# A padded row pitch for the V table in DRAM: 4608 bytes instead of 4160

## The chip, the core and the metric

The kernel runs on one core of one Trainium2 chip. The metric is device time in microseconds (us) of one execution. A core has a matrix engine (TensorE, "PE" in the profile; its weight loads are "PEld"), VectorE ("DVE"), ScalarE ("ACT"), GpSimd ("POOL") and SyncE ("SP"), which here only issues transfers, and 16 DMA engines that carry all transfers of the core. A matrix instruction reads SBUF and writes PSUM; DRAM is reached by DMA alone.

## What is computed

Block-sparse attention followed by a two-layer network with an ELU in between. From the reference, cut:

```python
B, H, S, D = 4, 8, 768, 64            # q, k, v: [B, H, S, D], float32
scores = q @ k^T / sqrt(D)            # per batch and head
# blocks of 32 positions, 24 of them; block i sees blocks i-1, i, i+1, the first, the last,
# and three blocks drawn at random for it (sampled_blocks[i]); blocks 0 and 23 see everything
attn = softmax(where(mask, scores, -1e9))
x = (attn @ v) as [B*S, H*D]          # 3072 x 512
h = x @ w_in                          # 512 -> 2048
out = where(h > 0, h, exp(min(h, 0)) - 1) @ w_out      # 2048 -> 512
```

## The kernel before, in words

The two batches of a pair and the two halves of a float32 number (a float16 high part and a float16 rest) are handled together. The work is cut into 24 units of attention (12 for each pair of batches; a unit has 128 query rows: two blocks of 32 for each of two batches) and 12 groups of the network (two units each). Units 0 to 3 and the first groups come while the weights are still being loaded, split and stored.

**The V table.** `vd[g]` in DRAM (L582, one for each pair of batches) holds V in the form in which the matrix engine reads it: 832 rows, one for a position; a row has both batches, all 8 heads, and for each the high part, two columns of ones and the rest: `2 * RW = 2080` float16 numbers, 4160 bytes. Row 0 to 31 are zero rows (for sampled blocks that are seen already), the first and the last block stand at the end of the table, and rows 736 to 767 are zero too (block 23's place in the sequence). It is written once:

- `zero_rows` (L584) clears a piece of SBUF (`ST`) and writes the zero rows of both tables with four transfers (L590).
- `first_values` (L648) splits V of the first pair in SBUF (`VT`) and writes it with five transfers (L666), two neighbouring rows, 8320 bytes, for each partition.
- `values` (L681) does the same for the second pair later, a row for each partition (L696).

It is read for every unit (`attention`, L733): for each of the two blocks of a unit one transfer on SP's queue brings the three neighbouring blocks (L803, 96 rows), and one indirect transfer that POOL issues brings 96 rows by their numbers in `idx` (L808). Two more direct transfers (L801, L802) bring the first and last block when a buffer is first used for a pair of batches. The two units that hold blocks 0 and 23 read the table whole (unit 0 from SBUF, unit 18 by L783 to L786). `idx` is built by `tables` (L441), the row number of each lane, as an integer.

**The order.** `Plan` is a list scheduler that runs when the program is built: each operation has the engines it may run on, estimated times and a priority, and the plan writes them down in the order in which a simulated machine would start them. Each engine then runs its list in order. SP's list is the order of the transfers in its queue; at most eight of SP's transfers are under way, since each waits for the one eight places before it (semaphores `DMAHW0` to `DMAHW7`).

At the start SP's list is: the sampled blocks, q of unit 0, eight loads of K (L621), six of V (L612; both in pieces of 512 bytes), the four writes of zero rows (L590), the first piece of `w_in` (L531) and of `w_out` (L535), the five writes of V (L666), three more q's, and so on. A piece of the weights is 1 MB and arrives as float32; `weights` (L504) turns it into two float16 halves: `wu` (L542, written by the helper at L393 on ACT), `ws` (L547), `wg` (L555), `wb` (L559) and so on.

Of the kernel before, what the change touches and what calls it, by code (L numbers as in the profile page):

```python
# [318 lines left out]
def kernel(  # L319
# [10 lines left out]
    nc = tc.nc  # L330
# [7 lines left out]
    NKC = S // P  # L338
    VW = 2 * D + 2
    RW = H * VW  # L340
    ROWS = (NB + 2) * BLK
    KW = (NR + 2) * BLK
    NPAIR = B // 2
# [97 lines left out]
    def tables():  # L441
        room = sb.tile([P, DM], F32, tag="ro.0", name="room")
        raw = room[:, 0 : 2 * NB * NR].bitcast(I32).rearrange("p (a b c) -> p a b c", b=NR, c=2)
        nc.sync.dma_start(
            raw.rearrange("p a b c -> p (a b c)"),
            sampled.bitcast(I32).rearrange("a b -> (a b)").partition_broadcast(P))
        t = room[:, 2 * NB * NR : 2 * NB * NR + 9 * NB].rearrange("p (a b) -> p a b", b=NB)
        sf = t[:, 0:3].rearrange("p a b -> p (a b)").rearrange("p (a b) -> p a b", b=NR)
        own, me, ok, k32 = t[:, 3], t[:, 4], t[:, 5], t[:, 6, 0:1]
        mi, ki = t[:, 7].bitcast(I32), t[:, 8, 0:1].bitcast(I32)  # L450
        nc.gpsimd.iota(mi, pattern=[[1, NB]], base=0, channel_multiplier=0)
        nc.gpsimd.iota(ki, pattern=[[0, 1]], base=0, channel_multiplier=1)
        nc.vector.tensor_copy(me, mi)
        nc.vector.tensor_scalar(ki, ki, BLK - 1, None, op0=ALU.bitwise_and)
        nc.vector.tensor_copy(k32, ki)
        nc.vector.tensor_copy(sf, raw[:, :, :, 0])
        nc.vector.tensor_scalar(
            col16[0:1, :].rearrange("p (a b) -> p a b", b=NR), sf[0:1], float(BLK // 2), None,
            op0=ALU.mult)
        for g in range(P // BLK):  # L460
            rs = slice(BLK * g, BLK * (g + 1))
            nc.vector.tensor_copy(own[rs], sf[rs, :, min(g, NR - 1)])
        nc.vector.tensor_tensor(me, own, me, op=ALU.subtract)
        nc.vector.tensor_tensor(me, me, me, op=ALU.mult)
        nc.vector.tensor_scalar(ok, me, WINDOW + 0.5, None, op0=ALU.is_gt)
        for e in (0.0, NB - 1.0):
            nc.vector.scalar_tensor_tensor(ok, own, e, ok, op0=ALU.not_equal, op1=ALU.mult)
        for g in range(1, NR):
            rs = slice(BLK * g, BLK * (g + 1))
            for r in range(g):  # L470
                nc.vector.tensor_tensor(me[rs], own[rs], sf[rs, :, r], op=ALU.not_equal)
                nc.vector.tensor_tensor(ok[rs], ok[rs], me[rs], op=ALU.mult)
        nc.vector.scalar_tensor_tensor(own, own, float(BLK), ok, op0=ALU.mult, op1=ALU.mult)
        nc.vector.tensor_scalar(idx, own, k32, None, op0=ALU.add)

    def turn16(t, src, dst, via, new=(), w=(), name="", bank="s", ml=ML):

# [101 lines left out]
    kT_buf = [[fixed(kT[:, :, x, c * P : (c + 1) * P]) for c in range(NKC)] for x in range(2)]  # L579
    kT_any = [b for x in kT_buf for b in x]  # L580
    kT_head = [Buf(None, None) for _ in range(H // 2)]
    vd = [buf("vd", [ROWS, 2 * RW], F16, dr) for _ in range(NPAIR)]  # L582

    def zero_rows(prio):  # L584
        z = spot("st4", lambda i: ST[:, i].bitcast(F16))
        plan.add({"POOL": 0.6}, prio, lambda e: nc.gpsimd.memset(z.ap[0:BLK, :], 0.0), new=[z], name="zero", port=False)
        for b in range(NPAIR):
            for n in (0, NB - 1):
                def put(e, b=b, n=n):
                    nc.sync.dma_start(vd[b].ap[n * BLK : (n + 1) * BLK, :], z.ap[0:BLK, :])  # L590
                plan.add({"SP": 0.45}, prio, put, r=[z], new=[vd[b]] if n == 0 else [],
                         w=[] if n == 0 else [vd[b]], dma=0.47, name=f"z{b}", pk=32)

# [54 lines left out]
    def first_values(a, js, prio, load, write):  # L648
        def slot():
            assert next_slot() == a  # L650
            return VT[:, 2 * a : 2 * a + 2].rearrange("p c b (h x) -> p c b h x", h=H)
        n = Buf("VT", slot)
        v_room.append(n)
        plan.add({"POOL": 0.5}, prio - 3, lambda e: nc.gpsimd.memset(
            n.ap.rearrange("p c b h x -> p (c b h) x")[:, :, D : D + 2], 1.0), new=[n], name=f"v10.{a}", port=False)
        for x in range(2):
            s, t = staged(js[x], v[x], a, load, f"v0.{a}")
            for c in range(2):
                split(prio, s, n, lambda x=x, c=c: n.ap[:, c, x, :, 0:D],
                      lambda x=x, c=c: n.ap[:, c, x, :, D + 2 :], VS, False, f"v0.{a}", t[:, :, c, :], mh=MHO)  # L660
        last = NB // (2 * P // BLK) - 1
        pieces = {0: [(0, HB, NB * BLK), (HB, P, BLK)],
                  last: [(0, P - HB, 2 * P * a), (P - HB, P, (NB + 1) * BLK)]}.get(a, [(0, P, 2 * P * a)])
        for p0, p1, row in pieces:
            def put(e, p0=p0, p1=p1, row=row):
                nc.sync.dma_start(  # L666
                    vd[0].ap[row : row + 2 * (p1 - p0), :].rearrange("(p c) e -> p (c e)", c=2),
                    n.ap[p0:p1].rearrange("p c b h x -> p (c b h x)"))
            mark["vs"] = plan.add({"SP": 0.43}, write, put, r=[n], w=[vd[0]], dma=2.7 * (p1 - p0) / P, name=f"vs0.{a}",
                     pk=256 * (p1 - p0) // P)  # L670

# [9 lines left out]
    def values(g, c, prio):  # L681
        n = spot("st4", lambda i: ST[:, i].bitcast(F16).rearrange("p (b h x) -> p b h x", b=2, h=H))
        plan.add({"POOL": 0.15}, prio, lambda e: nc.gpsimd.memset(n.ap[:, :, :, D : D + 2], 1.0),
                 new=[n], name=f"v1{g}.{c}", port=False)
        for x in range(2):
            s = buf("st2", [P, H, D], F32)
            plan.add({"SP": 0.9}, prio, lambda e, s=s, x=x: nc.sync.dma_start(
                s.ap, v[2 * g + x][:, c * P : (c + 1) * P, :].rearrange("h p d -> p h d")),
                new=[s], dma=2.0, name=f"v{g}.{c}", pk=1024)
            split(prio, s, n, lambda x=x: n.ap[:, x, :, 0:D], lambda x=x: n.ap[:, x, :, D + 2 :],  # L690
                  VS, False, f"v{g}.{c}")
        pieces = {0: [(0, BLK, NB * BLK), (BLK, P, BLK)],
                  NKC - 1: [(0, P - BLK, c * P), (P - BLK, P, (NB + 1) * BLK)]}.get(c, [(0, P, c * P)])
        for p0, p1, row in pieces:
            def put(e, p0=p0, p1=p1, row=row):
                nc.sync.dma_start(  # L696
                    vd[g].ap[row : row + p1 - p0, :], n.ap[p0:p1].rearrange("p b h x -> p (b h x)"))
            plan.add({"SP": 0.45}, prio, put, r=[n], w=[vd[g]], dma=1.8 * (p1 - p0) / P, name=f"vs{g}.{c}")


# [32 lines left out]
    def attention(u, t, via, due):  # L733
# [34 lines left out]
        elif sp:  # L768
# [7 lines left out]
            for c in range(NKC):  # L776
                vt = vts[c // 2]

                def load(e, c=c, vt=vt):
                    dst = VV[vt.slot][:, c % 2].rearrange("p b x -> p (b x)")  # L780
                    r0 = BLK + c * P
                    if c < NKC - 1:
                        nc.sync.dma_start(dst, vd[g].ap[r0 : r0 + P, :])  # L783
                    else:
                        nc.sync.dma_start(dst[0:64], vd[g].ap[r0 : r0 + 64, :])
                        nc.sync.dma_start(dst[64:P], vd[g].ap[NB * BLK :, :])  # L786
                plan.add({"SP": 0.5}, tv, load, r=[vd[g]], w=[vt], dma=1.9, name=f"vt{u}",
                         nd=1 if c < NKC - 1 else 2)
            vin = vts
        else:  # L790
            for y in range(2):
# [4 lines left out]
                def load(e, i=i, vt=vt, y=y):  # L796
                    vt.slot = 3 + y if u == spare else next_slot()
                    two = VV[vt.slot].rearrange("p c b x -> p c (b x)")
                    if in_room.get(("v", vt.slot)) != g:
                        in_room["v", vt.slot] = g  # L800
                        nc.sync.dma_start(two[96:P, 0, :], vd[g].ap[NB * BLK : (NB + 1) * BLK, :])  # L801
                        nc.sync.dma_start(two[0:BLK, 1, :], vd[g].ap[(NB + 1) * BLK :, :])  # L802
                    nc.sync.dma_start(two[BLK:P, 1, :], vd[g].ap[(i - 1) * BLK : (i + 2) * BLK, :])  # L803
                whole = u < spare + 2 or u == spare + 2 and y == 0
                plan.add({"SP": 1.5 if whole else 0.6}, tv, load, r=[vd[g]], new=[vt], dma=2.4 if whole else 1.45,  slack=RANK["SLACK"][2], name=f"vt{u}", nd=3 if whole else 1)

                def gather(e, i=i, vt=vt):
                    nc.gpsimd.indirect_dma_start(  # L808
                        VV[vt.slot][0:96, 0].rearrange("p b x -> p (b x)"), None, vd[g].ap,
                        bass.IndirectOffsetOnAxis(ap=idx[0:96, i : i + 1], axis=0))  # L810
                mark["vt", u] = plan.add({"POOL": 1.0}, tv, gather, r=[vd[g]], w=[vt], dma=1.65, slack=RANK["SLACK"][2], name=f"vg{u}")

# [377 lines left out]
```

## Time and profile before

| | |
|---|---|
| median of 3 runs | 736.94 us (734.59 to 737.84) |
| the profiled execution's own time | 739.45 us |
| its span, first to last instruction | 737.7 us |
| mean granted clock of TensorE | 0.964 |
| PE busy | 686.1 us (93%) |
| PEld, DVE, ACT, POOL busy | 461.7, 505.8, 442.2, 200.8 us |
| bytes moved | 125.26 MB, mean 170 GB/s |

The span begins with the first instruction, and all times inside the trace count from there. The 1.75 us between the span and the execution's own time lie around it. Share and busy time of an engine are means over stages with different limits, so the page's 40 slices and the stretches in the rows below say more.

### The profile page before, as it was taken

To read this page: it belongs to the slowest core of one execution; us is meant where nothing else is said; L and a number is where in the kernel's file an instruction comes from. 1 tells how busy PE (TensorE), PEld (TensorE's weight loads), DVE (VectorE), ACT (ScalarE), POOL (GpSimd) and SP (SyncE) were. 2 spreads that over 40 slices of the span, in tenths; PEclk is the share of its full clock that TensorE was granted. 3 is DMA by queue.
4 is the path that set the end of the run, shared out by engine and by line. 5 is a ranking of instruction groups with operands and counts; after the bars stand their busy time and mean duration, and the time that the engine had idled before them with its cause. 6 is when DMAs were issued, how large, how long until landed. Compare 5 with 4: busy or idle time off the path is not lost.

```text
span 737.7 us, 23053 instructions
## 1 busy us (share of the span) xinstructions
PE 686.1 (93%) x9377; PEld 461.7 (63%) x9377; DVE 505.8 (69%) x933; ACT 442.2 (60%) x867; POOL 200.8 (27%) x413
## 2 busy tenths in 40 slices
PE   7787666999999999999899899999999999999996
PEld 4565444866567677568468468576577477586662
DVE  7989698899988845758678657568466568352140
ACT  6886687786676744448458547546467456363340
POOL 2515226326513320410463323320033242100000
PEclk9689797999999999999999999999999999999999
DMA  9999979788889979788999897898659899621001
GB/s 235 312 282 267 296 216 240 173 190 186 223 129 209 193 184 223 161 200 128 204 139 186 134 201 170 129 212 165 112 99 218 166 167 191 137 44 23 21 1 28
DMA packets 221946, 125.26 MB, mean 170 GB/s; under 512 B 189008, under 2 KB 201424, under 8 KB 221456
## 3 DMA queue, kind: packets, MB, share of 16 engines
q1 hardware_dynamic: 216912, 106.22, 69.4%
q0 software_dynamic: 4928, 17.57, 9.3%
q8 instruction: 73, 1.20, 0.7%
q14 instruction: 33, 0.27, 0.1%
HBM read 76.99 MB, written 13.21 MB: 122 GB/s over the span
## 4 chain that ended last, share of the span: by engine, by line
PE 71%; DVE 8%; DMA 8%; ACT 5%; issue 4%; SPq 2%; POOL 1%; POOLq 1%; ACTq 0%; DVEq 0%
PE h L1057 29%; PE o L1083 26%; PE av L971 5%; PE s L883 5%; DMA pT<-p 2%; PE s L1083 2%; DMA VT<-vd 1%; ACT pT L393 1%; DMA wo<-in_k_dram 1%; DMA VT<-vd,idx 1%; DMA wi<-in_moe_w_in_dram 1%; DVE m L893 1%; DVE FE L1065 1%; SPq L621 1%; PE s L486 1%
## 5 line engine op out<-in xcount | busy, mean ns | idle before, releaser
L1057 PE MATMUL h<-xT,wi 128*128 128x256 f16 x2304 | 267.7, 274 | 3.1 <-DVE wi L566 1.6
L1057 PEld LDWEIGHTS <-wi 128*128 128x128 f16 x2304 | 223.2, 98 | 44.1 <-issue 6.6
L1083 PE MATMUL o<-wo,GR 128*128 128x512 f16 x1008 | 231.4, 379 | 1.3 <-ACT ro L393 0.7
L1083 PEld LDWEIGHTS <-GR 128*128 128x128 f16 x1152 | 108.1, 98 | 124.6 <-issue 7.7
L845 POOL COPY kG<-kT 128x128 int32 x264 | 94.6, 395 | 225.6 <-PE s L883 170.9
L1065 DVE SCALAR_TENSOR_TENSOR FE<-h,FE 128x512 f32<-128x512 f32 x96 | 65.7, 686 | 60.4 <-ACT FE L1070 60.3
L1068 ACT ACTIVATE FE<-h 128x512 f32<-128x512 f32 x96 | 56.8, 592 | 78.0 <-PE h L1057 77.8
L893 DVE TENSOR_REDUCE m<-s 128x2 f32<-128x512 f32 x112 | 75.1, 684 | 40.7 <-PE s L883 40.2
L919 ACT ACTIVATE e<-s,m 128x256 f32<-128x256 f32 x192 | 80.2, 471 | 19.3 <-DVE p L951 16.5
L393 ACT ACTIVATE GR<-FE 128x512 f16<-128x512 f32 x93 | 58.5, 629 | 43.4 <-DVE FE L1065 40.2
L1075 DVE TENSOR_TENSOR GR<-FE,GR 128x512 f16<-128x512 f32 x89 | 61.5, 694 | 26.7 <-ACT GR L393 26.0
L951 DVE TENSOR_TENSOR p<-e,p 128x512 f16<-128x512 f32 x81 | 57.6, 712 | 24.2 <-ACT p L393 19.8
L971 PEld LDWEIGHTS <-pT 128*32 128x32 f16 (+1 forms) x3816 | 49.3, 101 | 38.4 <-issue 35.3
L808 POOL DMA_INDIRECT VT<-vd,idx x42 | 45.3, 1078 | 96.6 <-PE av L971 76.1
L1070 ACT ACTIVATE FE<-FE,gs 128x512 f32<-128x512 f32 x96 | 69.2, 722 | 2.2
L971 PE MATMUL av<-VT,pT 128*32 128x66 f16 (+5 forms) x3624 | 57.8, 206 | 9.1 <-issue 5.3
L393 ACT ACTIVATE p<-e 128x512 f16<-128x512 f32 x74 | 46.1, 626 | 19.4 <-DMA pT<-p 19.2
L883 PE MATMUL s<-kG,qT 128*32 128x256 f16 x704 | 45.2, 281 | 5.8 <-ACT e L919 3.0
L883 PE MATMUL s<-kG,qS 128*32 128x256 f16 x704 | 44.7, 280 | 1.2 <-issue 0.7
L883 PEld LDWEIGHTS <-qT 128*32 128x32 f16 (+1 forms) x816 | 27.6, 100 | 27.0 <-issue 21.1
L393 ACT ACTIVATE ro<-o 128x512 f32<-128x512 f32 x19 | 11.3, 595 | 52.8 <-PE o L1083 52.8
L906 ACT ACTIVATE m<-m 128x2 f32<-128x2 f32 x91 | 18.3, 202 | 34.2 <-DVE m L893 31.0
(141 smaller groups left out, 683.6 us busy)
## 6 DMA issues: line engine op xcount, KB each, us to landing
VT<-vd SPq DMA_DIRECT2D x42, 390.0 KB, 7.2
st<-in_q_dram SPq DMA_DIRECT2D x44, 128.0 KB, 3.5
out_dram<-ro SPq DMA_DIRECT2D x44, 128.0 KB, 2.9
wi<-in_moe_w_in_dram SPq DMA_DIRECT2D x4, 1024.0 KB
wo<-in_k_dram SPq DMA_DIRECT2D x8, 384.0 KB, 6.3
wo<-in_v_dram SPq DMA_DIRECT2D x6, 512.0 KB, 6.9
wo<-in_moe_w_out_dram SPq DMA_DIRECT2D x3, 1024.0 KB, 5.1
st<-in_v_dram SPq DMA_DIRECT2D x12, 256.0 KB, 3.6
```

The source lines that it names most:

```text
L393: nc.scalar.activation(dst, src, AF.Copy, scale=scale)
L845: nc.gpsimd.tensor_copy(dst[:, :, r * 16 : (r + 1) * 16], src[:, :, bass.ds(at[r], 16)])
L883: nc.tensor.matmul(dst, lhsT=qq.ap[:, h, rs], rhs=mv, start=first, stop=(y == 1 and qq is qS and o0 + w == 256))
L893: nc.vector.tensor_reduce(m.ap[:, 2 * c : 2 * c + 2] if sp else m.ap[:, 6:8], ss[c].ap, axis=AX.X, op=ALU.max, negate=True)
L919: nc.scalar.activation(e32.ap[:, y, :], ss[c].ap[:, y, :], AF.Exp, bias=m.ap[:, 6 + y : 7 + y], scale=SC)
L951: plan.add(LO, t + step * hp + 1, margin=mo, fn=lambda e, got=got, p=p: ENG[e].tensor_tensor(p.ap[:, 1, :], got(), p.ap[:, 0, :], op=ALU.s ...
L971: nc.tensor.matmul(av[half].ap[rs, at : at + w], lhsT=pts[c].ap[:, pl * 4 + y * 2 + z, rs], rhs=room[:, z, x, h * VW + v0 : h * VW + v0 + ...
L1057: nc.tensor.matmul(h.ap[:, a, :], lhsT=w[:, wl, cs], rhs=x.ap[:, xl, cc, :], start=(n == 0), stop=(n == 3 * NCC - 1))
L1065: nc.vector.scalar_tensor_tensor(e32.ap, h.ap, -IH * GS, e32.ap, op0=ALU.mult, op1=ALU.min)
L1070: plan.add({"ACT": 0.72}, p0, lambda e: nc.scalar.activation(e32.ap, e32.ap, AF.Relu, bias=gs_col, scale=-GS), r=[e32], w=[e32], name=f"a2 ...
L1075: plan.add(LO, p0, margin=mo, fn=lambda e: ENG[e].tensor_tensor(g.ap[:, 1], e32.ap, g.ap[:, 0], op=ALU.subtract), r=[e32, g], w=[g], name= ...
L1083: nc.tensor.matmul(o.ap, lhsT=g.ap[:, gl, f % 2, m * P : (m + 1) * P], rhs=wo[:, part, wl, (f % 2) * DM : (f % 2 + 1) * DM], start=(f == 0 ...
```

## The change

A row of the table takes 2304 float16 numbers (`FAR`, 4608 bytes, nine times 512) in place of 2080; the 224 numbers (448 bytes) behind each row are padding. All reads and writes of rows take the first 2080 numbers of a row, so that every row that is moved begins at a multiple of 512 bytes (both tables begin at one before and after). The indirect transfers see the table in steps of 256 numbers, and `idx` holds nine times the row number: the last instruction of `tables` multiplies by 9 in the same instruction that adds. `zero_rows` issues one more transfer for each table, which writes zeros into the padding of all 832 rows. The writes of the first pair's V now have two pieces of 4160 bytes for each partition in place of one of 8320.

```diff
+    FAR = -(-2 * RW // 256) * 256
...
-        nc.vector.tensor_scalar(idx, own, k32, None, op0=ALU.add)
+        nc.vector.tensor_scalar(idx, own, k32, float(FAR // 256), op0=ALU.add, op1=ALU.mult)
...
-    vd = [buf("vd", [ROWS, 2 * RW], F16, dr) for _ in range(NPAIR)]
+    vd = [buf("vd", [ROWS, FAR], F16, dr) for _ in range(NPAIR)]
...
-                    nc.sync.dma_start(vd[b].ap[n * BLK : (n + 1) * BLK, :], z.ap[0:BLK, :])
+                    nc.sync.dma_start(vd[b].ap[n * BLK : (n + 1) * BLK, 0 : 2 * RW], z.ap[0:BLK, :])
+                    if n == 0:
+                        nc.sync.dma_start(
+                            vd[b].ap[:, 2 * RW :].rearrange("(p a) e -> p a e", p=BLK),
+                            z.ap[0:BLK, 0 : FAR - 2 * RW].unsqueeze(1).to_broadcast([BLK, ROWS // BLK, FAR - 2 * RW]))
...
-                    vd[0].ap[row : row + 2 * (p1 - p0), :].rearrange("(p c) e -> p (c e)", c=2),
-                    n.ap[p0:p1].rearrange("p c b h x -> p (c b h x)"))
+                    vd[0].ap[row : row + 2 * (p1 - p0), 0 : 2 * RW].rearrange("(p c) e -> p c e", c=2),
+                    n.ap[p0:p1].rearrange("p c b h x -> p c (b h x)"))
...
-                        nc.sync.dma_start(dst, vd[g].ap[r0 : r0 + P, :])
+                        nc.sync.dma_start(dst, vd[g].ap[r0 : r0 + P, 0 : 2 * RW])
...
-                        VV[vt.slot][0:96, 0].rearrange("p b x -> p (b x)"), None, vd[g].ap,
+                        VV[vt.slot][0:96, 0].rearrange("p b x -> p (b x)"), None, vd[g].ap.rearrange("r (a b) -> (r a) b", b=256),
```

The other transfers of rows (L696, L785, L786, L801 to L803) change as the one of L783 above. The estimates of the plan are untouched, and the order on PE, DVE, ACT and POOL is the same, instruction for instruction. SP's list gains the two transfers into the padding. Before, from the last load of V to the second write of V on SP (what a transfer writes, what it reads, its shape, and what SP waits for; `vd_425` and `vd_445` are the tables of the two pairs):

```order
L612 DMA wo<-in_v_dram 128x8x128 [waits DMAHW2_49,DVE_49]
L590 DMA vd_425<-ST 32x2080 [waits DMAHW3_49,Pool_49]
L590 DMA vd_445<-ST 32x2080 [waits DMAHW4_49]
L590 DMA vd_425<-ST 32x2080 [waits DMAHW5_49]
L590 DMA vd_445<-ST 32x2080 [waits DMAHW6_49]
L531 DMA wi<-in_moe_w_in_dram 128x4x512 [waits DMAHW7_49,PE_49]
L535 DMA wi<-in_moe_w_out_dram 128x2x1024 [waits DMAHW0_49,PE_49]
L666 DMA vd_425<-VT 112x4160 [waits DMAHW1_49,DVE_49]
```

With the change, the same stretch (the second table is now called `vd_446`, and lines from L339 on stand one to five further down):

```order
L617 DMA wo<-in_v_dram 128x8x128 [waits DMAHW2_49,DVE_49]
L591 DMA vd_425<-ST 32x2080 [waits DMAHW3_49,Pool_49]
L593 DMA vd_425<-ST 832x1x224 [waits DMAHW4_49]
L591 DMA vd_446<-ST 32x2080 [waits DMAHW5_49]
L593 DMA vd_446<-ST 832x1x224 [waits DMAHW6_49]
L591 DMA vd_425<-ST 32x2080 [waits DMAHW7_49]
L591 DMA vd_446<-ST 32x2080 [waits DMAHW0_49]
L532 DMA wi<-in_moe_w_in_dram 128x4x512 [waits DMAHW1_49,PE_49]
L536 DMA wi<-in_moe_w_out_dram 128x2x1024 [waits DMAHW2_49,PE_49]
L671 DMA vd_425<-VT 224x1x2080 [waits DMAHW3_49,DVE_49]
```

Two transfers of 832 pieces each now stand ahead of the first piece of `w_in`; everything behind them keeps its order and waits on semaphores two places further round.

## Rows read from the trace of the kernel before

**Rows 1.** The page's head, engines and 40 equal slices of the span.

```profile
span 737.7 us, 23053 instructions
PE 686.1 (93%) x9377; PEld 461.7 (63%) x9377; DVE 505.8 (69%) x933; ACT 442.2 (60%) x867; POOL 200.8 (27%) x413
PE   7787666999999999999899899999999999999996
DVE  7989698899988845758678657568466568352140
DMA  9999979788889979788999897898659899621001
```

**Rows 2.** Stretches: us, busy time of each engine (instructions), clock, DMA share, GB/s.

```profile
20.00:40.00 20.00, 14.43 (x111) 10.36 (x109) 19.23 (x35) 18.10 (x35) 9.72 (x22) 0.67 1.01 317
...
100.00:120.00 20.00, 11.49 (x292) 7.18 (x291) 17.78 (x30) 15.24 (x25) 6.62 (x16) 0.83 1.00 257
...
140.00:738.00 598.00, 581.68 (x7616) 389.06 (x7614) 387.56 (x725) 335.74 (x672) 150.41 (x307) 1.00 0.75 150
```

**Rows 3.** Chain of work that ended last: start, us, what (cut at 22 and 40).

```profile
23.50 1.37 SPq L590
...
26.50 7.08 DMA wi<-in_moe_w_in_dram
...
33.61 1.15 ACT wi L393
34.76 1.00 ACT wi L547
35.76 0.48 ACT pT L393
...
36.28 0.60 PE h L939
```

**Rows 4.** SP's queue in order of time: start, us, line, transfer, count.

```profile
23.25 3.15 SPq L590 DMA_DIRECT2D vd<-ST  x4
26.50 0.55 SPq L531 DMA_DIRECT2D wi<-in_moe_w_in_dram  x1
```

**Rows 5.** ACT in order of time; in brackets its idle time before, and what ended it.

```profile
33.61 1.15 ACT L393 ACTIVATE wi<-wi 128x1024 f32<-128x1024 f32 x1 [0.51 <-DMA wi<-in_moe_w_in_dram]
```

**Rows 6.** Short stretches in which nearly one kind of transfer runs (columns as in rows 2).

```profile
12.00:26.00 14.00, 10.40 (x108) 8.64 (x107) 11.80 (x20) 14.00 (x22) 4.99 (x11) 0.76 1.10 280
28.80:31.30 2.50, 1.13 (x9) 0.75 (x9) 2.19 (x4) 2.47 (x8) 2.09 (x6) 0.65 0.94 297
31.80:33.80 2.00, 2.00 (x19) 1.29 (x17) 2.00 (x4) 1.49 (x4) 1.09 (x2) 0.50 1.02 401
498.60:500.20 1.60, 1.60 (x17) 1.44 (x15) 1.60 (x4) 0.70 (x2) 0.82 (x1) 1.00 1.01 411
```

**Rows 7.** Queues over the whole span: packets, MB, share of 16 engines.

```profile
q1 hardware_dynamic: 216912, 106.22, 69.4%
q0 software_dynamic: 4928, 17.57, 9.3%
```

**Rows 8.** DMA issues: count, KB of each, median us to landing.

```profile
VT<-vd SPq DMA_DIRECT2D x42, 390.0 KB, 7.2
VT<-vd,idx POOLq DMA_INDIRECT x42, 7.3
```

**Rows 9.** Waits of PE for V, and of PE's weight loads for nothing seen: us, times, longest.

```profile
PE av L971 <- DMA VT<-vd: 1.8, 1, 1.8
PE av L971 <- DMA VT<-vd,idx: 0.8, 1, 0.8
PEld L971 <- issue: 35.3, 76, 4.4
PEld L883 <- issue: 22.1, 43, 3.8
```

**Rows 10.** Instructions on V's buffers from 140 us on: POOL's issues of the indirect transfers.

```profile
L808 POOL DMA_INDIRECT VT<-vd,idx x35: 909/944/1801, 154.0 to 635.1; - x35
```

More of the change, by code (lines that the diff above doesn't have):

```diff
@@ L696, in put @@
                 nc.sync.dma_start(
-                    vd[g].ap[row : row + p1 - p0, :], n.ap[p0:p1].rearrange("p b h x -> p (b h x)"))
+                    vd[g].ap[row : row + p1 - p0, 0 : 2 * RW], n.ap[p0:p1].rearrange("p b h x -> p (b h x)"))
             plan.add({"SP": 0.45}, prio, put, r=[n], w=[vd[g]], dma=1.8 * (p1 - p0) / P, name=f"vs{g}.{c}")
@@ L782, in load @@
                     if c < NKC - 1:
-                        nc.sync.dma_start(dst, vd[g].ap[r0 : r0 + P, :])
+                        nc.sync.dma_start(dst, vd[g].ap[r0 : r0 + P, 0 : 2 * RW])
                     else:
-                        nc.sync.dma_start(dst[0:64], vd[g].ap[r0 : r0 + 64, :])
-                        nc.sync.dma_start(dst[64:P], vd[g].ap[NB * BLK :, :])
+                        nc.sync.dma_start(dst[0:64], vd[g].ap[r0 : r0 + 64, 0 : 2 * RW])
+                        nc.sync.dma_start(dst[64:P], vd[g].ap[NB * BLK :, 0 : 2 * RW])
                 plan.add({"SP": 0.5}, tv, load, r=[vd[g]], w=[vt], dma=1.9, name=f"vt{u}",
@@ L800, in load @@
                         in_room["v", vt.slot] = g
-                        nc.sync.dma_start(two[96:P, 0, :], vd[g].ap[NB * BLK : (NB + 1) * BLK, :])
-                        nc.sync.dma_start(two[0:BLK, 1, :], vd[g].ap[(NB + 1) * BLK :, :])
-                    nc.sync.dma_start(two[BLK:P, 1, :], vd[g].ap[(i - 1) * BLK : (i + 2) * BLK, :])
+                        nc.sync.dma_start(two[96:P, 0, :], vd[g].ap[NB * BLK : (NB + 1) * BLK, 0 : 2 * RW])
+                        nc.sync.dma_start(two[0:BLK, 1, :], vd[g].ap[(NB + 1) * BLK :, 0 : 2 * RW])
+                    nc.sync.dma_start(two[BLK:P, 1, :], vd[g].ap[(i - 1) * BLK : (i + 2) * BLK, 0 : 2 * RW])
                 whole = u < spare + 2 or u == spare + 2 and y == 0
```

## The prediction

> **What bounds the kernel now.** I read the slices first, then the stretches, then the chain of waits, and last the rows of the V transfers. The slices [rows 1] show two stages. Up to about 130 us PE stands at six to eight tenths, while VectorE and the 16 DMA engines stand at nine or so; from 140 us on PE is full. The stretches put numbers to it [rows 2]: between 20 and 40 us VectorE is busy for 19.23 of 20 us and the DMA engines have a share of 1.01 (over 1 where packets of one engine overlap), and at 100 to 120 us both are still near that. From 140 us to the end PE is busy for 581.68 of 598 us, and the DMA share has fallen to 0.75. So there are two questions: what the change does to a full DMA queue and a full VectorE in the first stage, where each microsecond of delay is pushed on to the end; and whether a faster transfer of V rows is worth anything in the second, where PE works 97% of the time.
>
> The chain of waits answers most of the first. At its early end it runs through SP's issues of the zero rows, then for 7.08 us through the load of the first piece of `w_in`, then through what ACT does with that piece and through ACT's evictions into `pT`, for which PE waits [rows 3]. The reader is to see the 0.51 us in brackets [rows 5]: ACT has nothing left to do and stands at the instruction that needs the piece. Behind it on ACT stand the second pass over the piece and the `pT` copies of unit 0. This load has no slack.
>
> **The change part by part.**
>
> *The row number times 9* is a second operation in an instruction that is there anyway: nothing.
>
> *The padding.* The two new transfers stand in SP's list ahead of that load. SP issued the four zero writes at 23.25 us and the load at 26.50 [rows 4], when the DMA engines were busy with K and V loads and the queue was never empty: 12 to 26 us has a share of 1.10 [rows 6]. The load is 1 MB, which at the 297 to 401 GB/s that run just after its issue [rows 6] takes 2.6 to 3.5 us; it landed 7.08 us after its issue because it stood behind what was queued. So whatever is put ahead of it moves it by the time that this takes on the engines. That is 2 x 832 = 1664 pieces of 448 bytes, 0.745 MB. The nearest row is the stretch of 12 to 26 us, in which 512-byte pieces of K and V run at 280 GB/s [rows 6], which is 547 pieces per us. 1664 / 547 = 3.04 us if a piece costs the same, 0.745 MB / 280 GB/s = 2.7 us if the byte does. From above: the mean packet of SP's queue over the whole run occupies an engine for 0.694 x 16 x 737.7 us / 216912 = 37.8 ns [rows 7], which would make 1664 x 37.8 ns / 16 = 3.9 us. No row shows short pieces that go from SBUF to DRAM; a doubled price, 6.1 us, is a rival below. From below: nothing, if the engines had gaps that it fills; the share of 1.10 speaks against it. I take 3.0 us, since pieces of nearly the same length in the same stretch set it.
>
> SP's own issue time for the two (some 0.8 us each: the four zero writes took 3.15 us [rows 4]) lies beside this: the queue is full while SP issues. The same holds for the waits on the transfer eight places back: the load of `w_in` now waits for the fifth V load instead of the third from its end, and the next one for the last, which land before the engines come to them.
>
> What is late next: ACT stands for 3.5 us instead of 0.51, VectorE's next passes over the piece wait with it, and PE waits for `pT`. VectorE had 0.77 us of idle time in 20 to 40 us and little after [rows 2], so nothing makes the time good before 140 us; after that PE is full. I pass the 3.0 us on whole. Up to 1 us may be lost or won on the way: PE's granted clock is down to 0.67 in this stretch already, and another gap of 3 us on PE may keep it there.
>
> *The first pair's V in 4160-byte pieces.* 384 pieces of 8320 bytes become 768 of 4160, 3.2 MB. Rows of 4160 bytes run at 411 GB/s (next part), so the writes stay where they are to within a few tenths of a microsecond, and unit 1 reads them much later. Nothing.
>
> *The rows that begin at multiples of 512.* This is the part that could win. The 42 direct reads of 390 KB [rows 8] move 16.8 MB and POOL's queue 17.57 MB [rows 7], together 34 of the 125 MB, so a few per cent there would be visible in the DMA share. But look at 498.6 to 500.2 us [rows 6]: almost only the loads of whole 128-row pieces run, from rows that begin at every multiple of 64, and they move 411 GB/s at a share of 1.01. From 31.8 to 33.8 us the second megabyte of weights runs, in pieces of 4096 bytes at multiples of 512, and moves 401 GB/s at 1.02. Rows that begin anywhere already go as fast as rows that begin at 512. The 7.2 and 7.3 us from issue to landing [rows 8] are therefore queue and latency: 390 KB at 411 GB/s is 0.97 us. And PE waits for V only 1.8 + 0.8 = 2.6 us in the whole run [rows 9]. Bounds: between 0 and -2.6 us; I take 0, by the two stretches.
>
> [...]
>
> **Sum:** 0 + 3.0 + 0 + 0 = +3.0 us. The profiled execution took 739.45 us, so it would take 742.4; it lies 2.5 us above the median of the runs, 736.94, and on the median the sum gives 739.9 us.
>
> **The rivals.**
>
> *Short writes cost double.* If a 448-byte piece that is written to DRAM takes twice what a 512-byte piece takes on its way to SBUF, the two transfers hold the queue for 6.1 us and the time is 743.0 us. [...]
>
> *The load is late and nobody minds.* ACT has 1.90 us of idle time in the 20 us around this load [rows 2], and if such gaps go on behind it and are waits for something that is not late, the delay is swallowed step by step. The time would stay at 737. Against it stands a VectorE with 0.77 us of idle time in 20, which has the rest of the piece's passes to do.
>
> *Faster.* The mechanism would be the shared engines. PE's weight loads wait 35.3 + 22.1 us for nothing that the trace names, in 119 pieces of up to 4.4 us [rows 9]; new instructions reach PE over the same engines as V. If rows at 512 cut the time of a V packet among other traffic, code and transposes come sooner. It decides the sign once it saves more than the 3.0 us, that is over 5% of these 57.4 us, and it gives a gain that counts (3.7 us) at 6.7 us, 12% of them: 733 us. For it: the share of V in the bytes, over a quarter. Against: the 411 GB/s, which leave no room on an engine that is alone.
>
> *The change doesn't do what it says.* The indirect transfer sees a table in steps of 512 bytes. If its 4160 bytes are then moved in pieces of 512, 44 x 96 pieces become nine times as many, 33,800 more, at 547 per us 62 us of engine time. Each gather would land 1.4 us later. After 140 us the engines are free for a quarter of the time [rows 2] and 35 of the gathers lie there [rows 10]; the nine before it meet a full queue, 9 x 1.4 = 12.6 us. With the 3.0 us that is 752 us.
>
> **How the numbers follow.** A measurement of this kernel can tell about 0.5%, 3.7 us, from no change. The chances: the forecast (+1.5 to +4.5 us) 0.50, short writes at double price 0.20, swallowed 0.17, faster 0.08, pieces of 512 bytes 0.05. Of the forecast's 0.50 some 0.34 lies under +3.7 us. Within 0.5%: 0.34 + 0.17 = 0.51; slower: 0.16 + 0.20 + 0.05 = 0.41, rounded to 0.40; faster 0.08, rounded to 0.09. The range reaches from 735.5 (swallowed, with a little won on the waits for V) to 744.5 us (double price with the clock's microsecond and a half) and leaves out the faster rival and the pieces of 512 bytes.
>
> **What the next profile would show.** Right: the load of `w_in` lands at about 36.6 instead of 33.6 us, with ACT idle for some 3.5 us before it; packets of SP's queue up by 1664 and 384; the stretch with only whole V loads still at about 410 GB/s; V to landing still near 7 us; the stretch of full PE begins 3 us later and is as long as before. A landing at 39 us speaks for the double price; ACT's gap without a later end, for the swallowed delay; a packet count of the other queue near 39,000, for the pieces of 512 bytes. Wrong altogether would be a shorter stretch after 140 us, with less of PE's unnamed waits.

## The result and the profile after

The kernel with the padded pitch takes 744.04 us, median of 20 runs (737.18 to 747.93), the one before 739.40 us, also of 20 (733.95 to 747.88). The ratio is 1.0056 (95%: 1.0032 to 1.0081), so the change costs 4.1 us, with an interval of 2.4 to 6.0. Here and below, ratios and the microseconds worked out from them leave out executions over 1.5% longer than the fastest of their kernel, while the medians hold them. On the median of the first three runs, 736.94 us, the ratio gives 741.1 us against 739.9 forecast; the twenty runs of the kernel before have a median 2.46 us above those three, which is most of why 744.04 lies so near the upper end of the range. The profiled execution took 741.13 us.

The page's head, engines and slices after the change:

```profile
span 739.4 us, 23055 instructions
PE 682.5 (92%) x9377; PEld 458.6 (62%) x9377; DVE 506.5 (68%) x933; ACT 441.6 (60%) x867; POOL 201.2 (27%) x413
...
PE   7677676999999899999999999999999999999996
...
DVE  7979788999988756658678757668467568452140
...
DMA  9999999987889999889988897897559999721001
...
q1 hardware_dynamic: 218992, 106.97, 69.6%
q0 software_dynamic: 4928, 17.57, 9.8%
```

Against [rows 1] the busy times are nearly what they were; PE's is 3.6 us less. SP's queue q1 has 218992 packets instead of 216912 [rows 7], 2080 more: the 1664 pieces of padding, 384 from the first pair's V, and 32. POOL's queue still has 4928 packets, so an indirect transfer still moves its row in one piece. That count also places the 32: 44 transfers of 96 rows leave 4928 - 4224 = 704, 16 for each transfer, and two transfers were added (e2 below has 218608 packets, 1696 more than the kernel before, so 848 = 832 + 16 for each). Now the chain of work that ended last, around the load of the first piece of `w_in` (start, us, what):

```profile
30.55 6.54 DMA wi<-in_moe_w_in_dram
37.09 0.02 issue
37.11 1.10 ACT wi L394
38.21 0.99 ACT wi L548
39.20 0.49 ACT pT L394
39.69 0.04 issue
39.73 0.60 PE h L944
```

It is the chain of [rows 3], 3.5 us later: ACT begins the piece at 37.11 instead of 33.61, PE's matmul into `h` comes at 39.73 instead of 36.28. SP's queue and then ACT, in order of time, show where it comes from (start, us, what; in brackets idle time before, and what ended it):

```profile
23.16 1.65 SPq L591 DMA_DIRECT2D vd<-ST  x1
24.86 0.71 SPq L593 DMA_DIRECT2D vd<-ST  x1
25.62 0.68 SPq L591 DMA_DIRECT2D vd<-ST  x1
26.35 1.75 SPq L593 DMA_DIRECT2D vd<-ST  x1
28.14 2.31 SPq L591 DMA_DIRECT2D vd<-ST  x2
30.55 0.97 SPq L532 DMA_DIRECT2D wi<-in_moe_w_in_dram  x1
...
37.11 1.10 ACT L394 ACTIVATE wi<-wi 128x1024 f32<-128x1024 f32 x1 [3.92 <-DMA wi<-in_moe_w_in_dram]
```

The two L593 are the new transfers. SP comes to the load at 30.55 instead of 26.50 [rows 4], and ACT stands for 3.92 us at the instruction at which it stood for 0.51 [rows 5]. The stretches (us, busy time of PE, PEld, DVE, ACT, POOL with instructions, clock, DMA share, GB/s):

```profile
28.00:31.00 3.00, 0.74 (x9) 0.53 (x9) 2.62 (x7) 2.47 (x7) 1.51 (x3) 1.00 0.87 220
31.00:33.50 2.50, 2.50 (x21) 1.53 (x20) 2.50 (x5) 2.19 (x5) 1.40 (x5) 0.53 0.85 182
140.00:740.00 600.00, 581.95 (x7633) 389.67 (x7630) 390.03 (x728) 337.74 (x677) 152.20 (x309) 1.00 0.75 150
20.00:40.00 20.00, 11.58 (x102) 8.66 (x99) 15.90 (x31) 15.39 (x27) 9.48 (x22) 0.76 0.99 282
500.90:502.50 1.60, 1.60 (x17) 1.43 (x15) 1.60 (x5) 1.23 (x2) 0.14 (x1) 1.00 1.04 377
```

From 20 to 40 us VectorE is busy for 15.90 us instead of 19.23, ACT for 15.39 instead of 18.10, PE for 11.58 instead of 14.43 [rows 2]: all three lost about 3 us. From 28 to 31 us, while the padding is written (1166 of 1203 packets are under 512 bytes), the queue moves 220 GB/s at a share of 0.87, where K and V moved 280 at 1.10 [rows 6]; the zero rows and the first of the weights follow at 182 GB/s. From 140 us on PE has 581.95 us of work, as before (581.68). In the stretch with the loads of whole 128-row pieces the now aligned rows run at 377 GB/s, where the unaligned ones ran at 411 [rows 6]. Such a stretch is too short to weigh the two: begun 0.4 us earlier or later it gives 335 and 359 here, 367 and 403 before. Transfers of V from issue to landing, and PE's waits (count, KB, median us; us, times, longest):

```profile
VT<-vd SPq DMA_DIRECT2D x42, 390.0 KB, 5.7
VT<-vd,idx POOLq DMA_INDIRECT x42, 7.6
...
PEld L976 <- issue: 33.0, 74, 4.5
```

The direct loads land after 5.7 us instead of 7.2 [rows 8], which looks like a gain by alignment until the experiments below show 5.5 us with the old pitch (e2) and 7.1 with the new one (e3). PE's weight loads still wait 33.0 us for nothing seen (35.3 before [rows 9]). For the prediction's remark that new instructions come over the engines of V, the page of the kernel before has two queues of instructions beside SP's and POOL's (packets, MB, share of 16 engines):

```profile
q8 instruction: 73, 1.20, 0.7%
q14 instruction: 33, 0.27, 0.1%
```

Which engine they feed, and whether PE's weight loads wait for them, is not shown.

### The profile page after: what moved, and what is told of

Its sections match the earlier page's. It is cut to its first block, busy times and chain, and to the rows that moved or that the text cites. A ratio compares the mean times of both kernels' runs of the same rounds, so it can differ in the third digit from the quotient of the medians.

```text
span 739.4 us, 23055 instructions
## 1 busy us (share of the span) xinstructions
PE 682.5 (92%) x9377; PEld 458.6 (62%) x9377; DVE 506.5 (68%) x933; ACT 441.6 (60%) x867; POOL 201.2 (27%) x413
## 3 DMA queue, kind: packets, MB, share of 16 engines
q1 hardware_dynamic: 218992, 106.97, 69.6%
q0 software_dynamic: 4928, 17.57, 9.8%
## 4 chain that ended last, share of the span: by engine, by line
PE 72%; DVE 8%; DMA 8%; ACT 6%; issue 4%; POOL 1%; POOLq 1%; SPq 0%; DVEq 0%; ACTq 0%
PE h L1062 29%; PE o L1088 27%; PE av L976 5%; PE s L888 5%; DMA pT<-p 3%; DMA wi<-in_moe_w_in_dram 2%; DVE m L898 1%; DMA VT<-vd 1%; PE s L1088 1%; ACT kT L394 1%; PE warm L433 1%; DMA VT<-vd,idx 1%; ACT pT L394 1%; DVE FE L1070 1%; PE s L487 1%
## 5 line engine op out<-in xcount | busy, mean ns | idle before, releaser
L976 PEld LDWEIGHTS <-pT 128*32 128x32 f16 (+1 forms) x3816 | 47.7, 99 | 39.4 <-issue 33.0
L976 PE MATMUL av<-VT,pT 128*32 128x66 f16 (+5 forms) x3624 | 56.2, 203 | 10.6 <-issue 5.9
L911 ACT ACTIVATE m<-m 128x2 f32<-128x2 f32 x91 | 18.4, 203 | 35.0 <-DVE m L898 31.6
```

Of the source, the lines that this page charges most:

```text
L976: nc.tensor.matmul(av[half].ap[rs, at : at + w], lhsT=pts[c].ap[:, pl * 4 + y * 2 + z, rs], rhs=room[:, z, x, h * VW + v0 : h * VW + v0 + ...
```

## The experiments

My theory: the time goes to the 1664 pieces that stand ahead of the first `w_in` load, and the pitch itself is worth nothing. The rivals: the pitch costs (or gives) something by itself; short pieces are written at a doubled price; the delay would be swallowed; or the pieces cost wherever they stand in the first stage, and not by this load alone.

**The padding without the pitch (e2).** The kernel before, table as it was; two transfers of the same shape and place write into scratch memory.

```diff
+    far = [dr.tile([ROWS, 2304], F16, tag=f"far.{i}", name=f"far{i}") for i in range(2)]
...
+                    for x in far[1 * b : 1 * (b + 1)] if n == 0 else []:
+                        nc.sync.dma_start(
+                            x[:, 2 * RW :].rearrange("(p a) e -> p a e", p=BLK),
+                            z.ap[0:BLK, 0:224].unsqueeze(1).to_broadcast([BLK, ROWS // BLK, 224]))
```

> The kernel before, with two added transfers of 832 pieces of 448 bytes at the place where the change has them, but into a scratch tensor; V table, its pitch and all reads as before. The scratch is never read. First theory (what is put ahead of the first load of w_in moves that load, ACT stands for it, and the delay goes through to the end): the load lands at about 37 us in place of 33.6, ACT stands about 3.5 to 4 us before it, time +3 to +4 us, ratio about 1.005. Rival (the new pitch, or V's writes in smaller pieces, cost the time): ratio 1.000, the load late or not.

Measured: 743.63 against 739.88 us, 1.004 (1.0004 to 1.0076). ACT in order of time:

```profile
37.78 1.10 ACT L393 ACTIVATE wi<-wi 128x1024 f32<-128x1024 f32 x1 [4.81 <-DMA wi<-in_moe_w_in_dram]
```

The landing is 4.2 us late, the time 3.0 us longer (0.3 to 5.6). The padding alone gives a loss of the change's size. Beside 1.0056 for the whole change this leaves 0.16% for the pitch, and the two intervals together (roots of the summed squares) make that plus or minus 0.44%: nothing that can be told. The 42 direct loads of V here, with 4160-byte rows:

```profile
VT<-vd SPq DMA_DIRECT2D x42, 390.0 KB, 5.5
```

So 5.7 us after the change need not be the alignment's doing. In this execution VectorE also stands for 4.69 us at the second piece of `w_in` (64.54 us), which it does neither before nor after the change.

**The padding three times (e4).** As e2 with six transfers, three where one was: 4992 pieces.

> As the fill alone, but six added transfers into scratch tensors in place of two (4992 pieces of 448 bytes). First theory: the load of w_in lands about 9 to 10 us late, near 43 us, and the end moves by as much, ratio 1.012 to 1.014: the delay is passed on in proportion. Rival (a delay is swallowed in part, and two fills happen to cost what they cost): under 1.009. If a short piece written to DRAM costs double, the landing would be near 52 us.

Measured: 752.13 against 739.88 us, 1.0154 (1.0097 to 1.021) from six runs, so 11.4 us longer (7.2 to 15.5). ACT, and the long stretch in which almost only padding is written (columns as above):

```profile
45.31 1.10 ACT L393 ACTIVATE wi<-wi 128x1024 f32<-128x1024 f32 x1 [12.16 <-DMA wi<-in_moe_w_in_dram]
```

```profile
28.00:38.00 10.00, 5.26 (x33) 3.54 (x33) 7.36 (x16) 4.66 (x11) 3.26 (x8) 0.66 0.83 197
```

And the transfers of 27.5 to 38 us by size, with SP's queue (packets, MB, share of the 16 engines); last, SP's queue before the change from 12 to 26 us, where K and V are loaded:

```profile
DMA packets 4486, 2.12 MB, mean 202 GB/s; under 512 B 4437, under 2 KB 4449, under 8 KB 4483
q1 hardware_dynamic: 4483, 2.09, 83.3%
...
q1 hardware_dynamic: 7753, 3.91, 109.3%
```

The landing moves by 11.7 us and the end by 11.4: within its interval the delay is passed on whole. It is 1.95 us for each transfer of 832 pieces, 3.9 us for two. 4437 pieces in 10.5 us are 423 per us, not the 547 that I took from K and V. A piece does not hold its engine longer: 0.833 x 16 x 10.5 us / 4483 are 31.2 ns for a packet here, 1.093 x 16 x 14 us / 7753 are 31.6 ns for one of K and V. The engines' share is 0.83 instead of 1.10, and the lower rate is that lower share: gaps, or less overlap between packets. A doubled price would be 3.04 us for each transfer and a landing near 52 us: refuted.

**The padding behind the first weights (e3).** The whole change, but the two transfers are held back and issued right after the first loads of `w_in` and `w_out`.

```diff
-                        nc.sync.dma_start(
+                        late.append(lambda: nc.sync.dma_start(
...
+                while late:
+                    late.pop(0)()
```

> The changed kernel, its two fills of the padding issued behind the first loads of w_in and w_out in place of ahead of them; the same work and pitch. First theory: the load of w_in lands at 33.6 us again, ACT stands under 1 us, and the time is that of the kernel before, ratio 1.000 (0.997 to 1.003), though the writes of V come about 3 us later. Rival one (the pitch costs): still 1.005 or 1.006. Rival two (any 3 us of extra work in the full DMA queue come back at the end, wherever they stand): still 1.004 to 1.006.

Measured: 741.53 against 739.88 us, 1.0006 (0.9966 to 1.0045). ACT:

```profile
34.37 1.13 ACT L394 ACTIVATE wi<-wi 128x1024 f32<-128x1024 f32 x1 [1.28 <-DMA wi<-in_moe_w_in_dram]
...
48.53 0.63 ACT L394 ACTIVATE n<-st 128x512 f16<-128x512 f32 x1 [0.87 <-DMA st<-in_q_dram]
```

The same pieces, the same pitch, another place in the list: the wait is 1.28 us and no loss can be told. The ratio lies 0.50% under the change's, give or take 0.46 (worked out as for e2), so the order matters, but only just clear of the noise; under e2's it lies 0.34%, give or take 0.53. Its interval reaches 1.0045, so a part of the price may remain at the new place. It doesn't show a gain by the pitch either. Part of the delay has gone to the next load, q of a later unit, for which ACT waits 0.87 us.

**Padding late in the program (e8).** The kernel before, and six transfers into scratch memory of e4's shape (from another piece of SBUF), in pairs behind the q loads of units 14 to 16, near 380 us.

```diff
+        if not store and u in (14, 15, 16):
+            for x in spare_t[2 * (u - 14) : 2 * (u - 13)]:
+                fill(x)
```

> The kernel before, with six fills of 832 pieces of 448 bytes into scratch tensors (the amount of the kernel with three times the fill, which measured 1.0154), issued in pairs behind the loads of q of units 14, 15 and 16, some 350 to 410 us into the run, where PE is full and the DMA engines are not. The scratch is never read. First theory (place decides, not the amount): ratio 1.000 to 1.002. Rival (9 us of engine time come back wherever they are spent): 1.010 or more.

Measured: 747.91 against 741.59 us, ratio 1.0046 (1.0008 to 1.0083). Beyond that place nothing is read from its profile. The same 4992 pieces cost 3.4 us (0.6 to 6.2) in place of 11.4: the place decides most of the price, but I had expected next to none. The DMA engines aren't as free there as I took them to be: from 350 to 410 us their share is 0.89 in the kernel before, with PE busy for 57.25 of 60 us.

**The four zero writes behind the first weights (e5, repeated).** If whatever stands ahead of the load costs, the kernel before should get faster by moving its own zero rows back. No pitch, no padding.

```diff
-                    nc.sync.dma_start(vd[b].ap[n * BLK : (n + 1) * BLK, :], z.ap[0:BLK, :])
+                    late.append(lambda: nc.sync.dma_start(vd[b].ap[n * BLK : (n + 1) * BLK, :], z.ap[0:BLK, :]))
...
+                while late:
+                    late.pop(0)()
```

> The kernel before, its four writes of zero rows (128 pieces of 4160 bytes) issued behind the first loads of w_in and w_out; nothing added. First theory: the load of w_in lands 1.3 to 2 us earlier, near 32 us, ACT's wait of 0.51 us is gone, and since ACT and VectorE are nearly full then, the time falls by 0.5 to 2 us, ratio 0.998 (0.996 to 1.000). Rival (the load's place matters only once it is late, ACT's other work ends last): ratio 1.000, with ACT's wait gone and the same time.

> The kernel before with its zero rows behind the first loads of weights, a second time, on the chip of the two others so that the three can be set beside each other: 0.9956 again (0.993 to 0.999); a ratio of 1.000 or more would say that its first measurement was chance.

Measured: 736.59 against 739.88 us, 0.9956 (0.9926 to 0.9987), and on another chip 741.41 against 742.56, 0.9973 (0.9937 to 1.0008). The first has the only interval of all these runs that lies wholly below no change; the repeat's does not. ACT no longer waits for the piece of `w_in`, but then for q, and VectorE for the second piece:

```profile
32.80 1.19 ACT L393 ACTIVATE wi<-wi 128x1024 f32<-128x1024 f32 x1
...
46.67 0.63 ACT L393 ACTIVATE n<-st 128x512 f16<-128x512 f32 x1 [1.52 <-DMA st<-in_q_dram]
...
57.53 0.76 DVE L397 TENSOR_SCALAR wi<-wi 128x1024 f32<-128x1024 f32 x1 [3.48 <-DMA wi<-in_moe_w_in_dram]
```

Before, neither stood at these two (no brackets):

```profile
48.04 0.68 ACT L393 ACTIVATE n<-st 128x512 f16<-128x512 f32 x1
...
55.50 0.70 DVE L397 TENSOR_SCALAR wi<-wi 128x1024 f32<-128x1024 f32 x1
```

**Pitch with everything behind (e6).** The change, with zero rows and padding both held back as in e3 and e5; if the pitch gives something, it should show here without the delay.

> The changed kernel, with the four writes of zero rows and the two fills all issued behind the first loads of w_in and w_out. Against the kernel with only its zero rows moved so (4160 bytes of pitch), which measured 0.9956, it differs in the pitch and the fills alone. First theory (the pitch is worth nothing, the fills are hidden there): ratio 0.996, between 0.993 and 1.000, the first pass over the weights on ACT at about 33 us with no wait for the load. Rival (aligned rows save time that the fills had eaten): 0.993 or less. Rival (the fills cost wherever they stand, since V's writes and the next loads come 3 us later): 1.000 or more.

Measured: 742.63 against 741.59 us, 1.0014 (0.9981 to 1.0048): no gain, and 0.58% above e5 (give or take 0.45; 0.41 and 0.49 against the repeat), which differs by pitch and padding. That is what I had set down as a rival: the padding costs here too, though it stands behind the first weights, and about as much as ahead of them. Pitch and padding are not separated in this pair. The delay stands at q and at the second piece of `w_in`:

```profile
50.04 0.63 ACT L394 ACTIVATE n<-st 128x512 f16<-128x512 f32 x1 [2.97 <-DMA st<-in_q_dram]
...
60.08 0.69 DVE L398 TENSOR_SCALAR wi<-wi 128x1024 f32<-128x1024 f32 x1 [2.57 <-DMA wi<-in_moe_w_in_dram]
```

**Further back: e7, e11, e12.** Is there a place in the first stage where the extra writes are free? e7 is e6 with zero rows and padding behind the q loads of units 1 to 3 (`while late and not store and u == 3`). e11 is e5 with the zero rows behind q of unit 1 (`u == 1`). e12 is e5 with the q loads of units 2 and 3 behind the second load of `w_in`, so that VectorE gets its piece earlier.

> The changed kernel (4608 bytes of pitch), zeros and fills issued behind the first loads of weights, V's writes and the loads of q of units 1 to 3. Theory (the pitch is worth nothing; the fills cost what they make late, here the second load of w_in and the first V reads, by about 3 us, which have a few us of slack): 0.998 (0.994 to 1.002), ACT without a wait for w_in and for q of unit 1. Rival (the pitch wins once the fills are out of the way): 0.993 or less. Rival (3 us in a full queue cost 3 us): 1.002 or more.

> The kernel before (4160 bytes of pitch, no fills), its four writes of zero rows issued behind the first loads of weights, V's writes and the load of q of unit 1. With the zeros only behind the weights, ACT no longer waited for w_in but stood 1.52 us for this q. Theory (each load in the front of SP's queue has a consumer that stands for it, so what can wait goes behind those that can't): ACT's wait for q is under 0.5 us, ratio 0.994 (0.991 to 0.998). Rival (only the first load of weights matters, q is not on the path): the same as with the zeros behind the weights, 0.9956. Rival (what is gained early is lost at the second load of w_in, which the same bytes still precede): 0.998 to 1.000.

> The kernel before with its zero rows behind the first loads of weights, and in addition the loads of q of units 2 and 3 behind the second load of w_in. With the zeros alone moved, VectorE stood 3.3 to 3.5 us for this second load (57.5 us). Theory (in the front of the queue the load that somebody stands for decides, one after the other): VectorE's wait at the second load falls under 2 us, ratio 0.992 (0.988 to 0.996). Rival (the front is bound by the sum of the bytes, and the next load in line is late instead, q of units 2 and 3): 0.996 to 0.998, with a new wait on ACT or VectorE for q of about the same length.

Measured: e7 748.59 against 742.56 us, 1.0067 (1.0035 to 1.0098); e11 741.92 against 742.56, 0.9986 (0.9947 to 1.0026); e12 744.45 against 742.00, 1.0049 (1.0014 to 1.0083). VectorE's waits in e7, in e11 and in e12:

```profile
64.72 0.69 DVE L398 TENSOR_SCALAR wi<-wi 128x1024 f32<-128x1024 f32 x1 [8.56 <-DMA wi<-in_moe_w_in_dram]
```

```profile
62.76 0.69 DVE L397 TENSOR_SCALAR wi<-wi 128x1024 f32<-128x1024 f32 x1 [4.21 <-DMA wi<-in_moe_w_in_dram]
```

```profile
52.55 0.43 DVE L397 TENSOR_SCALAR n<-st 128x512 f16<-128x512 f32 x1 [2.96 <-DMA st<-in_q_dram]
```

None came out as its theory had it; e7 and e11 match the last of their rivals. In e7 the second piece of `w_in` is what all six transfers hold up, and against e11, which has neither pitch nor padding, the ratio is 0.81% higher, give or take 0.51: the price is there again. In e11 ACT's wait for q, which was to go under 0.5 us, is 2.79 us (e7: 3.08), longer than in e5 though nothing was put ahead of that load; why stays open. In e12 the wait for the second piece is gone and one for q has come in its place, but the time is above the kernel before, which neither theory nor rival had. The loads looked at in this part of the list each have an engine that stands for them, and moving something back hands the wait to another; the length of the waits alone does not give the time, since e11 waits longer than the kernel before and takes as long.

## Why the prediction came out as it did

- **The place of the loss: right for the padding ahead of the load.** ACT's wait grew from 0.51 to 3.92 us, the padding without the pitch (e2) has the loss, and padding by dose gives 0, 4.2 and 11.7 us of landing delay for none, two and six transfers. Undoing the order alone (e3) leaves 1.0006. That the loss needs this one load is not shown: behind it, in e6 and e7, the padding (with the pitch) cost 0.4 to 0.8% against e5 and e11.
- **The size of the term: too small at the landing.** The landing came 3.50 us late after the change, 4.2 in e2, 3.9 for each pair in e4, where the sum had 3.0; the loss itself, 2.4 to 6.0 us, does not tell 3.0 from these. The step "since pieces of nearly the same length in the same stretch set it" holds by engine time, 31.2 ns a packet against 31.6. What failed is "the queue is full while SP issues": the engines' share falls from 1.10 to 0.87 after the change and 0.83 in e4, and 423 pieces go per us where the sum had 547. The upper bound of 3.9 us was met by chance, since it came from longer packets and not from a lower share. What lowers the share wasn't separated: SP's issue (0.71 and 1.75 us for the two here, 0.61 and 0.89 in e7), the 32 source partitions or the writes to DRAM.
- **Nothing swallows it: right, as far as the intervals tell.** 11.4 us at the end (7.2 to 15.5) for 11.7 at the landing in e4, 3.0 (0.3 to 5.6) for 4.2 in e2, 4.1 (2.4 to 6.0) for 3.5 after the change. The profiled pair of before and after shows less: the first and last network matmul of the two (start times in us, after "to" the last) are

```profile
L1057 PE MATMUL h<-xT,wi x2304: 269/273/421, 92.6 to 710.9; 128*128 128x256 f16 x192
```

```profile
L1062 PE MATMUL h<-xT,wi x2304: 269/273/421, 95.8 to 712.7; 128*128 128x256 f16 x192
```

  so the delay is 3.2 us at the first and 1.8 at the last, and the spans differ by 1.7. Single executions of one kernel lie 10 us and more apart, so this pair doesn't weigh against twenty runs. The microsecond that the prediction kept for the clock did not show: from 20 to 40 us PE's granted clock is 0.76, not below the 0.67 of before [rows 2], and its mean is 0.971 against 0.964.
- **Aligned rows worth nothing: right as far as can be told.** 377 GB/s against 411 for whole loads; no run with the new pitch came out below the kernel before, and e2 beside the change leaves 0.16%, plus or minus 0.44. The two stretches are too rough to rule out a difference of a few per cent: begun 0.4 us earlier or later they give from 335 to 377 GB/s here and from 367 to 411 before.
- **Writes at double price: wrong.** e4 shows 1.95 us for 832 pieces, 1.3 times the 1.52 of the sum (3.04 / 2) and not twice, and no more time on the engine for each piece (31.2 ns against 31.6 for one of K and V).
- **The indirect transfers: right.** 4928 packets before and after.
- **A misreading without effect.** By its semaphore the load of `w_in` waited before for the fourth load of V from the end, not the third.
- **What the sum couldn't say:** by which side of 0.5% it ends. The forecast's own size, 3.0 us, lay under that border; the measured 0.56% lies just over it, and its interval spans it.

A pitch of 4608 bytes with no padding written at all wasn't tried: the view of the indirect transfer covers the padding, which would be memory that nothing has written.

## What to carry to other kernels

Before a layout is changed for alignment, look for a stretch in which transfers that begin anywhere run alone: if they already move what aligned ones move, there is little to win, as here (411 GB/s against 401 [rows 6]). Price what a change adds to a queue by what stands behind it, not by its bytes: here two small transfers ahead of a load for which an engine stands cost their whole time on the queue (the load 3.50 us late, the end 4.1). Behind it they were not free by themselves: once no loss could be told (1.0006 in e3), but in e6 and e7 the next loads waited and the price came back (0.58% and 0.81% above e5 and e11), and only far from the first stage did six transfers cost clearly less (3.4 us in e8, 11.4 in e4). Moving the four zero writes out of the load's way gave 0.4%, in a repeat 0.3% that no change could also give, and two further moves built on it did not keep it.

## What the runs showed that was not expected

- Pieces of 448 bytes written to DRAM bring the 16 engines to a share of only 0.83 and move 197 GB/s over 10 us (e4), against 280 GB/s at 1.10 for 512-byte loads [rows 6]. A packet holds its engine as long as one of K and V, 31.2 and 31.6 ns, so the lower rate is the lower share and not longer pieces.
- Extra writes near 380 us, in the stage where PE is full (581.68 of 598 us [rows 2]), still cost 3.4 us for six transfers (e8). Which load they delay there stays open.
- The median time from issue to landing of the same 42 loads is 7.2 us in the profiled execution before and 5.5 in e2's, both with the old pitch, and 5.7 after the change and 7.1 in e3's, both with the new one: it can't tell one pitch from the other.
